# Starting the preparation of three attention units three steps later

## The chip, the cores and the metric

The kernel runs on one core of one Trainium2 chip. The time is the device time of that core in microseconds (us), the median of several executions. Five engines work beside each other, each through its own list of instructions in order: TensorE (PE in the profile), ScalarE (ACT), VectorE (DVE), GpSimd (POOL) and SyncE (SP), which here issues DMAs and DMA transposes. They wait for each other through semaphores.

## The reference

Normalised attention, then a feed-forward block with a residual, over 8 batches of 448 tokens, 12 heads of 64 and a model width of 768. Cut to what is computed:

```
q_n = q / sqrt(mean(q*q) + 1e-6) * g_q          (k_n likewise with g_k)
attn = softmax(q_n @ k_n.T / sqrt(64))
x = (attn @ v), heads side by side               (8, 448, 768), float32
xn = (x - mean(x)) / sqrt(var(x) + 1e-6) * g_ln
out = x + relu(xn @ w_ch1) @ w_ch2               w_ch1: 768 x 3072, w_ch2: 3072 x 768
```

## The kernel before, in words

**Pairs and units.** Attention works on pairs of heads: 48 pairs, six to a batch. The inputs of one or two pairs are loaded and prepared together as a unit. From unit 4 on a unit holds two pairs: unit 5 has pairs 8 and 9, unit 6 has 10 and 11, unit 7 has 12 and 13, unit 8 has 14 and 15, unit 9 has 16 and 17.

**Steps.** After a first stretch whose order is written out by hand, attention is a list of steps, numbered 7p + i for pair p and i = 0 to 6. Step 7p + i emits the scores of part i of pair p (S, lines 352 to 356, then the exponential on ScalarE at line 358) and the product with v of the pair before it (V, lines 381 and 383). The steps are dealt out among the chunks of the MLP of the batch before: an up chunk is six matmuls into psH (line 621) and a Relu on ScalarE (line 623); a down chunk is six matmuls into psC (line 637). While the MLP of batch 0 runs, it takes the steps up to 90 with it. The last 13 down chunks carry no steps; beside them the layer norm of the next batch is made on VectorE (lines 545, 560, 566) and transposed by DMA into xnT (line 593), which the up chunks of the next MLP read.

**Preparation of a unit.** It is cut into twelve pieces, which are put into the steps ahead of the scores of that step:

- `bai`: takes the buffers, squares k on ScalarE into the buffer khl (line 215), and multiplies k by the gains on GpSimd (line 229)
- `d`, `c`, `e`: sum of the squares of k on VectorE (line 218), squares of q on ScalarE into the buffer qn (line 215), their sum on VectorE
- `j`: the high half of k on ScalarE (line 237)
- `gv`: the roots on ScalarE (lines 221, 223), v on GpSimd
- `k`, `l`, `m`: the low half of k, the scaled q and its copy on VectorE (lines 240, 67, 279)
- `w`: the rest of v on GpSimd
- `x`, `y`, from unit 8 on: DMA transposes of khl and qn into kU and qU (lines 258, 261, 268, 271)

For units below 8, PE transposes khl and qn in place of `x` and `y`: K for pair p + 1 stands in step 7p + 2 (lines 313, 316) and Q for pair p + 1 in step 7p + 4 (lines 327, 330), both into one PSUM buffer tr, which VectorE copies out (lines 318, 335).

**Buffers.** khl and qn have two buffers each. A buffer that a unit takes is one that an earlier unit has been done with; its first writer is a square of ScalarE, which waits for the last reader of the earlier unit. The scores have two PSUM buffers psS: the scores of a step wait for the exponential of two steps before.

**Where the pieces stand.** A unit has a first step `st` and a last step `e`, and the ten pieces from `bai` to `w` are spread evenly between them; the rule and the table of exceptions:

```
st = max(7 * (p - 2 - m) + 2, last + 1, 7 * nb0)
e = max(7 * (p - 2) - 1, st + 5)
st, e = EARLY.get(u, (st, e))
...
at = st + (e - st) * x // (k - 1) if x < k else e + 1 + x - k
```

The order of PE, ScalarE, GpSimd and SyncE is that in which the steps emit; that of VectorE after the first stretch is chosen when the program is built. The load of the second half of `w_ch2` (`load_w2`, line 520, issued by GpSimd) is emitted in the step of unit 7's `bai`.

Of the kernel before, what the change touches and what calls it, by code (L numbers as in the profile page):

```python
# [45 lines left out]
""".split()  # L46
DMA_UNIT = 8
PE_SET = (DMA_UNIT + 1) % 2
EARLY = {5: (42, 49), 6: (47, 56)}
LN_EXP_SET = 6  # L50
UP_FIRST = 3
REC_LO, REC_HI = 1.0 / 3.0e7, 0.5
# [23 lines left out]
class _Fast:  # L76
# [381 lines left out]
    def attention(self):  # L458
# [3 lines left out]
        for u in range(4, nu):  # L462
            p, m = UNIT_PAIR[u], UNITS[u][2]
# [3 lines that stand above are left out]
            pieces = ["bai", "d", "c", "e", "j", "gv", "k", "l", "m", "w", "x", "y"]  # L467
# [469 lines left out]
```

## Time and profile before

| | |
|---|---|
| time, median of 3 | 615.18 us (614.29 to 615.19) |
| span of the profiled execution | 613.1 us |
| PE busy | 580.8 us (95%) |
| ScalarE, VectorE, GpSimd busy | 361.4, 286.8, 188.2 us |
| mean granted TensorE clock | 0.995 |

A line of a timeline has the start and the length in us, engine and source line, the operation, what it writes and reads, and in brackets the idle time of the engine ahead of it with what ended it. A line of the waits has who waited for whom: us in total, how often, the longest. A line of the windows has a stretch of time, and the busy time of each engine in it; PEclk is the share of full TensorE clock that was granted. PEld is the loading of weights, which overlaps PE.

### The profile page before, as it was taken

To read this page: it belongs to the slowest core of one execution; us is meant where nothing else is said; L and a number is where in the kernel's file an instruction comes from. 1 tells how busy PE (TensorE), PEld (TensorE's weight loads), DVE (VectorE), ACT (ScalarE), POOL (GpSimd) and SP (SyncE) were. 2 spreads that over 40 slices of the span, in tenths; PEclk is the share of its full clock that TensorE was granted. 3 is DMA by queue.
4 is the path that set the end of the run, shared out by engine and by line. 5 is a ranking of instruction groups with operands and counts; after the bars stand their busy time and mean duration, and the time that the engine had idled before them with its cause. 6 is when DMAs were issued, how large, how long until landed. Compare 5 with 4: busy or idle time off the path is not lost.

```text
span 613.1 us, 11532 instructions
## 1 busy us (share of the span) xinstructions
PE 580.8 (95%) x4500; PEld 346.3 (56%) x4500; DVE 286.8 (47%) x618; ACT 361.4 (59%) x697; POOL 188.2 (31%) x245
## 2 busy tenths in 40 slices
PE   2887999799999999999999999999999999999995
PEld 1555566455566666655566666655566666654564
DVE  5898566633356356643346355642355422440011
ACT  5996986338754498538755398537765377214200
POOL 2852621223452245514453145605322000000000
PEclk9999999899999999999999999999999999999999
DMA  9999999275766477847665496838523330030011
GB/s 193 272 212 207 213 221 189 31 222 134 122 109 128 117 123 150 180 106 144 105 108 141 107 136 151 176 104 151 119 59 87 91 61 2 27 104 0 1 52 56
DMA packets 130861, 75.29 MB, mean 123 GB/s; under 512 B 96656, under 2 KB 121040, under 8 KB 130800
## 3 DMA queue, kind: packets, MB, share of 16 engines
q1 hardware_dynamic: 114048, 45.12, 37.5%
q0 software_dynamic: 16080, 28.94, 21.1%
q8 instruction: 37, 0.61, 0.4%
q10 hardware_dynamic: 672, 0.43, 0.2%
q14 instruction: 24, 0.20, 0.1%
HBM read 52.36 MB, written 11.01 MB: 103 GB/s over the span
## 4 chain that ended last, share of the span: by engine, by line
PE 82%; DVE 2%; DMA 2%; ACT 2%; issue 1%; SPq 1%; DVEq 0%; ACTq 0%
PE psC L637 34%; PE psH L621 33%; PE psS L352 7%; PE oA L381 4%; PE oB L383 2%; PE psS L355 1%; PE psS L356 1%; DMA qkv<-in_k_dram 1%; DMA kU<-khl 1%; ACT E L358 1%; ACT qn L215 0%; DVE qn L67 0%; DVE stat L545 0%; DVE khl L240 0%; ACT khl L215 0%
## 5 line engine op out<-in xcount | busy, mean ns | idle before, releaser
L621 PE MATMUL psH<-xnT,w 128*128 128x512 f16 (+1 forms) x1134 | 241.9, 353 | 0.3 <-ACT hT L671 0.3
L637 PE MATMUL psC<-w,hT 128*128 128x384 f16 (+1 forms) x1368 | 235.6, 324 | 0.0
L358 ACT ACTIVATE E<-psS,rr_all 128x448 f16<-128x448 f32 x336 | 206.9, 635 | 47.8 <-PE psS L352 42.6
L623 ACT ACTIVATE hT<-psH 128x512 f16<-128x512 f32 (+1 forms) x189 | 104.1, 551 | 124.4 <-PE psH L621 121.6
L637 PEld LDWEIGHTS <-hT 128*128 128x128 f16 x1368 | 128.1, 98 | 74.8 <-issue 0.7
L621 PEld LDWEIGHTS <-w 128*128 128x128 f16 x1134 | 102.7, 98 | 81.2 <-issue 0.8
L352 PE MATMUL psS<-qU,kU 128*128 128x448 f16 x288 | 100.9, 358 | 10.9 <-ACT E L358 8.9
L381 PEld LDWEIGHTS <-E 128*128 128x128 f16 x1008 | 70.9, 98 | 51.0 <-issue 7.0
L229 POOL TENSOR_TENSOR qkv<-qkv,gprod 128x896 f32<-128x896 f32 x21 | 43.7, 2079 | 99.4 <-ACT khl L215 60.5
L381 PE MATMUL oA<-v,E 128*128 128x65 f16 x864 | 66.9, 194 | 0.1
L641 DVE SCALAR_TENSOR_TENSOR x<-psC,rs_all,x 128x384 f32<-128x384 f32 x48 | 28.9, 615 | 71.7 <-PE psC L637 71.2
L396 DVE RECIPROCAL rec_all<-oA 128x6 f32<-128x6 f32 x48 | 9.3, 194 | 96.6 <-PE oA L381 96.4
L383 PE MATMUL oB<-v,E 128*128 128x65 f16 x288 | 51.9, 194 | 0.1
L127 POOL DMA_DIRECT2D qkv<-in_k_dram x14 | 11.2, 797 | 129.7 <-ACT E L358 67.9
L218 DVE TENSOR_REDUCE ssq<-khl 128x14 f32<-128x896 f32 (+1 forms) x24 | 25.6, 1065 | 48.7 <-ACT khl L215 48.6
L352 PEld LDWEIGHTS <-kU 128*128 128x128 f16 x288 | 28.3, 99 | 24.6 <-issue 6.2
L218 DVE TENSOR_REDUCE ssq<-qn 128x14 f32<-128x896 f32 (+1 forms) x25 | 26.2, 1047 | 25.1 <-ACT qn L215 25.1
L67 DVE SCALAR_TENSOR_TENSOR qn<-qkv,rq 128x256 f16<-128x256 f32 (+1 forms) x72 | 26.5, 424 | 18.0 <-ACT rq L223 17.9
L383 PEld LDWEIGHTS <-E 128*128 128x128 f16 x336 | 32.5, 97 | 0.3 <-DVE xl L403 0.2
L398 DVE TENSOR_TENSOR x<-oA,rec_all 128x384 f32<-128x384 f32 x48 | 26.8, 558 | 1.5
L545 DVE BATCH_NORM_STATS2 stat<-x 128x6 f32<-128x256 f32 (+1 forms) x75 | 26.3, 405 | 0.7
L240 DVE TENSOR_TENSOR khl<-qkv,khl 128x896 f16<-128x896 f32 x21 | 22.8, 1087 | 7.1 <-ACT khl L237 6.3
(104 smaller groups left out, 446.7 us busy)
## 6 DMA issues: line engine op xcount, KB each, us to landing
out_dram<-x SPq DMA_DIRECT2D x20, 384.0 KB, 2.5
qkv<-in_k_dram POOLq DMA_DIRECT2D x14, 384.0 KB, 3.8
qkv<-in_q_dram POOLq DMA_DIRECT2D x14, 384.0 KB, 5.4
qkv<-in_v_dram POOLq DMA_DIRECT2D x14, 384.0 KB, 6.5
w<-in_moe_w_ch_dram POOLq DMA_DIRECT2D x3, 1536.0 KB, 14.5
w<-in_moe_w_ch_dram POOLq DMA_DIRECT2D x2, 2304.0 KB, 27.0
qkv<-in_k_dram SPq DMA_DIRECT2D x7, 384.0 KB, 5.7
qkv<-in_q_dram SPq DMA_DIRECT2D x7, 384.0 KB, 5.1
```

The costliest lines, as they stand in the source:

```text
L67: nc.vector.scalar_tensor_tensor(out=out, in0=x, scalar=8.0, in1=r.unsqueeze(2).broadcast_to([x.shape[0], g, D]), op0=ALU.mult, op1=ALU.mult)
L218: nc.vector.tensor_reduce(out=c["ssq"][:, n], in_=c["sq", n], axis=AX.X, op=ALU.add)
L229: (nc.vector if u in DVE_KG else nc.gpsimd).tensor_tensor(out=c["t"][1], in0=c["t"][1], in1=sh.gprod.unsqueeze(1).broadcast_to([128, g, D] ...
L352: nc.tensor.matmul(ps[:, 0:S], c["main"][:, ts(i, 128)], q[:, ts(h, S)], start=True, stop=True)
L358: nc.scalar.activation(out=c["E"][:, i], in_=ps[:, 0:S], func=AFT.Exp, scale=self.rr[:, g:g + 1], bias=EXP_BIAS)
L381: nc.tensor.matmul(oA[:, t, cs], E[:, i, ts(t, 128)], rhs, start=(i == 0 and t == 0), stop=(i == 6 and t == 2))
L383: nc.tensor.matmul(oB[:, cs], E[:, i, 320:448], rhs, start=(i == 0), stop=(i == 6))
L398: nc.vector.tensor_tensor(out=x[:, :, 128 * hp:128 * hp + 128].rearrange("p t (e d) -> p t e d", e=2), in0=oA[:, :, :, 0:D], in1=rec[:, 0: ...
L621: nc.tensor.matmul(ps[:, 0:N], sh.w1[:, dc, ts(f, 128)], xnT[:, dc, 0:N], start=(dc == 0), stop=(dc == NDC - 1))
L623: nc.scalar.activation(out=hT[:, f, 0:N], in_=ps[:, 0:N], func=AFT.Relu)
L637: nc.tensor.matmul(ps[:, 0:g[1]], hT[:, f, ts(t, 128)], sh.w2[:, f, cols], start=(f == 0), stop=(f == NFF - 1))
L641: nc.vector.scalar_tensor_tensor(out=x[:, cols], in0=ps[:, 0:g[1]], scalar=self.rs[:, b, t:t + 1], in1=x[:, cols], op0=ALU.mult, op1=ALU.add)
```

## The change

Units 7, 8 and 9 get an entry in the table of exceptions, each three steps after the rule's value, with the same last step. It is meant to put the first square behind the PE transposes that read the buffers which the unit takes, where before it stood ahead of them in the order of steps.

```diff
-EARLY = {5: (42, 49), 6: (47, 56)}
+EARLY = {5: (42, 49), 6: (47, 56), 7: (61, 69), 8: (75, 83), 9: (89, 97)}
```

The rule gave (58, 69), (72, 83) and (86, 97). So the pieces move as follows, and those of units 8 and 9 the same way 14 and 28 steps later:

| unit 7 | bai | d | c | e | j | gv | k | l | m | w |
|---|---|---|---|---|---|---|---|---|---|---|
| step before | 58 | 59 | 60 | 61 | 62 | 64 | 65 | 66 | 67 | 69 |
| step after | 61 | 61 | 62 | 63 | 64 | 65 | 66 | 67 | 68 | 69 |

The transposes K and Q of the pair 9 stand in steps 58 and 60, those of pair 11 in 72 and 74, those of pair 13 in 86 and 88. The pieces `x` and `y` of unit 8 stay in steps 84 and 85. No operation is added or taken away.

## The prediction

> **What bounds the kernel now.** I read the page first, then PE's waits in the stretch that holds steps 58 to 90 (about 71 to 116 us), then the timelines of ScalarE, PE and SyncE around the longest of them.
>
> ```profile
> PE 580.8 (95%) x4500; PEld 346.3 (56%) x4500; DVE 286.8 (47%) x618; ACT 361.4 (59%) x697; POOL 188.2 (31%) x245
> ...
> PE   2887999799999999999999999999999999999995
> ...
> PE psC L637 34%; PE psH L621 33%; PE psS L352 7%; PE oA L381 4%; PE oB L383 2%; PE psS L355 1%; PE psS L356 1%; DMA qkv<-in_k_dram 1%; DMA kU<-khl 1%; ACT E L358 1%; ACT qn L215 0%; DVE qn L67 0%; DVE stat L545 0%; DVE khl L240 0%; ACT khl L215 0%
> ```
>
> PE sets the end. It is full from the ninth slice to the end but the last, so a microsecond that PE loses before is a microsecond of the total. The seventh of the 40 slices above (92 to 107 us) is full, the eighth (107 to 123 us) is not: digit 7 stands there. PE's waits from 55 to 155 us:
>
> ```profile
> PE psS L352 <- ACT E L358: 3.5, 3, 2.7
> PE tr L327 <- DVE kU L318: 1.4, 2, 0.7
> PE psS L355 <- ACT E L358: 0.6, 2, 0.3
> ```
>
> One wait of 2.7 us carries most. Now the six squares of units 7, 8 and 9 in ScalarE's timeline:
>
> ```profile
> 72.41 0.95 ACT L215 ACTIVATE khl<-qkv 128x896 f32<-128x896 f32 x1 [0.21 <-PE tr L316]
> ...
> 75.37 0.95 ACT L215 ACTIVATE qn<-qkv 128x896 f32<-128x896 f32 x1 [0.20 <-PE tr L330]
> ...
> 89.10 0.95 ACT L215 ACTIVATE khl<-qkv 128x896 f32<-128x896 f32 x1
> ...
> 92.06 0.95 ACT L215 ACTIVATE qn<-qkv 128x896 f32<-128x896 f32 x1 [0.20 <-DMA qkv<-in_k_dram]
> ...
> 109.17 0.95 ACT L215 ACTIVATE khl<-qkv 128x896 f32<-128x896 f32 x1 [3.70 <-DMA kU<-khl]
> ...
> 112.86 0.95 ACT L215 ACTIVATE qn<-qkv 128x896 f32<-128x896 f32 x1 [1.69 <-DMA qU<-qn]
> ```
>
> Units 7 and 8 wait 0.2 us for PE's transposes; that is little. Unit 9 waits 3.7 us, and not for PE: K of pair 13 had ended at 106.7 us. It waits for the DMA transposes of unit 8, so unit 9 took the buffers of unit 8, which had been given back (steps 84, 85) ahead of those of unit 7 (K in step 86, Q in 88). SyncE's timeline shows these transposes[...]:
>
> ```profile
> 98.10 3.69 SPq L258 DMA_TRANSPOSE kU<-khl  x1
> 101.84 2.50 SPq L261 DMA_TRANSPOSE kU<-khl  x2
> 104.44 4.68 SPq L268 DMA_TRANSPOSE qU<-qn  x3
> 109.17 2.52 SPq L271 DMA_TRANSPOSE qU<-qn  x2
> ```
>
> The chain has the last landing of kU<-khl 5.96 us after 103.11, at 109.07, which is when the square begins. And PE:
>
> ```profile
> 106.88 1.14 PE L637 MATMUL psC<-w,hT 128*128 128x384 f16 x6
> 110.70 0.35 PE L352 MATMUL psS<-qU,kU 128*128 128x448 f16 x1 [2.68 <-ACT E L358]
> 110.89 0.25 PE L381 MATMUL oA<-v,E 128*128 128x65 f16 x3
> 110.97 0.19 PE L383 MATMUL oB<-v,E 128*128 128x65 f16 x1
> 111.86 0.27 PE L327 MATMUL tr<-id,qn 128*128 128x128 f16 x1 [0.69 <-DVE kU L318]
> 111.92 0.84 PE L330 MATMUL tr<-id,qn 128*128 128x128 f16 x6
> 112.56 2.12 PE L637 MATMUL psC<-w,hT 128*128 128x384 f16 x6
> ```
>
> The square stood in step 86 ahead of the exponential of S12.2. Blocked, it held up that exponential; the scores of step 88 wanted its psS buffer, and PE stood. The sum of the squares (VectorE, line 218) in turn stood ahead of the copy of tr, so Q of pair 13 came another 0.7 us late. And the six psC matmuls then took 1.92 us in the chain, not 0.97.
>
> **What the Trainium skill says.** "TensorE: Matmul & The Clock Gate", part 1, has the array at half clock after an idle window of about 3.4 us, and at full clock only after as long a busy one. The trace agrees: the windows give PEclk 0.50 from 112 to 115 us, after some 2.7 us of idleness and a broken microsecond. The same page, "Architectural detail", has ScalarE and VectorE as strict first-in first-out queues; here the blocked square held the exponential behind it. "ScalarE: Activation LUTs", "What ACT_TABLE_LOAD costs", prices an activation with immediate operands at 186 ns + 0.833 ns an element: 932 ns for 896, and the trace has 949.
>
> **The change part by part.**
>
> *Unit 9.* Its `bai` goes from step 86 to 89 and `c` from 88 to 90. The exponentials of S12.2, S12.3 and S12.4 then stand ahead of the square, so the scores of step 88 (buffer of S12.2), step 89 (S12.3) and step 90 (S12.4) find theirs free whatever the square waits for. The next scores, step 91, come after the 13 chunks without steps, 12.68 us later. So the wait is not taken away but has nobody behind it. What PE does between the end of psC at 107.85 us and the first of those chunks at 115.92 took 8.07 us. At full clock and without waits, from equal pieces in the chain: S 0.19, V 0.12, Q 0.41, psC 0.97, S and V 0.31, the split scores and V of step 90 0.61; 2.61 us in all. Gain 5.46 us: 2.85 of the first gap, 0.8 of the second, the rest slow clock and small gaps.
>
> *Units 7 and 8.* The squares leave the places before S8.2, S8.4, S10.2 and S10.4. Two short waits of PE follow on qn squares (0.28 at 76.89 us, 0.27 at 93.58 us). Gain 0.55 us.
>
> *What comes closer together.* Unit 7's two squares and the high half, each 0.84 us of ScalarE when queued closely, now stand in steps 61, 62 and 64 in place of 58, 60 and 62. ScalarE was busy 4.80 of 5 us from 75 to 80. Going through its queue from 72 us with an exponential at 0.52, a Relu at 0.37: it falls about 2 us behind at S9.1 and catches up by S9.4, with scores of steps 62 to 67 each finding their buffer free by 0.1 to 0.6 us. So 0 to 1 us of new stalls; I take 0.3. Unit 8's run stands where PE does down chunks, which need no Relu (ScalarE 3.28 of 5 us from 95 to 100), and costs nothing. The copy of tr for pair 12 may fall behind unit 8's low half on VectorE; 0 to 0.4 us, taken in the 0.3.
>
> *The rest of the preparation* ends in the same step or one later. Its readers are far: K of pair 12 in step 79, S14.0 in step 98. The `w_ch2` load is issued about 3 us later, from 75.5 to some 78.5, behind the first half that was still filling the queue (24 us to landing); its first user is the second column half of psC, at about 111 us, some 4 us after the landing at 106.8 (issue done at 77.0, 30 us to landing). Nothing.
>
> *The layer norm of batch 1.* It hangs on V of step 90, so it moves up with PE. Before, V ended at 115.9, the transposes into xnT were issued up to 125.2 and the last landed about 126.5; PE wanted it at 128.4. Slack 1.9 us. After: unit 8's transposes go one step (1.2 us) later, kU landing at about 110.3; square to 111.2, its sum on VectorE to 112.3; if that stands ahead of the copies out of step 90 (ready at 110.5), the chain starts 1.8 us late, inside the slack. 0 to 1.5 us; I take 0.2.
>
> Sum: 615.18 - 5.46 - 0.55 + 0.3 + 0.2 = 609.67 us. From 130 us on PE is full (69.87 of 70 us from 130 to 200), so nothing gives it back.
>
> **The rivals.**
>
> *The layer norm becomes the wait.* If VectorE also has unit 9's second sum ahead of the copies of step 90, the chain waits for the landing of qU<-qn, 112.8 + 1.2 = 114.0, plus square 0.95 and sum 1.1: copies at 116.0, as before. xnT lands at 126.6, PE stands from 123.0 to 126.6 and starts slow (about 1.6 us, as above). Gain 0.2 to 1.8: 613.8 us. For it: VectorE's order is chosen at build. Against: before, the low half of unit 9 was ready in time and still stood behind the whole layer norm.
>
> *The wait moves with the square.* PE stands in step 89 or 90 as it did in 88; only the 0.55 us remain: 614.6 us. For it: unit 9 would still take unit 8's buffers. Against: the count of psS buffers above.
>
> *Slower: the denser burst.* Unit 7 stalls PE for 1 us, the layer norm waits 3.6 us with 1.6 us of slow clock, and unit 8 adds 0.6 by the copy of tr: 5.46 + 0.55 - 6.8 = -0.8, and 616 us. For it: ScalarE's 96% from 75 to 80 us. Against: all three must come together.
>
> **How the numbers follow.** Forecast 0.75, layer norm 0.12, moved wait 0.07, slower 0.06. The forecast's own bounds are 609.2 (no new stall) to 611.7 (1 and 1.5 us of them); the median before moved by 0.9 us between executions, so the low end is 608.6. Above 613.4 lie the moved wait, the slower case and half the layer-norm case, 0.19. Faster by 0.2% means under 613.95: 0.75 and over half of 0.12, 0.82. Same 0.09, slower 0.09.
>
> **What would show it.** Right: no wait of PE for ScalarE over 0.5 us near 105 to 112 us; PEclk 1.00 there; unit 9's first square about 109 to 111 us, with a wait or none; first psH of 128x512 at about 122.6 to 123.2 us. ScalarE's squares of unit 7 at about 75.5 and 77.3 us. Wrong: PE waiting for xnT before that psH, a wait of psS for E in steps 61 to 67 over 0.5 us, or a new gap after 130 us.

## The result, and the profile after

| | before | after |
|---|---|---|
| time, median of 4 (us) | 615.18 (614.29 to 615.63) | 609.68 (608.87 to 610.34) |
| ratio, 95% interval | | 0.9912 [0.9893, 0.993] |
| span of the profiled execution (us) | 613.1 | 608.4 |
| part of the chain that PE carries | 82% | 88% |

The change takes 5.5 us off; the forecast was 609.7. First the page of after, with the lines that answer to those of before, and the clock:

```profile
PE 579.9 (95%) x4500; PEld 346.0 (57%) x4500; DVE 286.4 (47%) x618; ACT 360.5 (59%) x697; POOL 188.8 (31%) x245
...
PE   2886999999999999999999999999999999999995
...
PEclk9899999999999999999999999999999999999999
...
PE 88%; ACT 1%; DVE 0%; issue 0%; ACTq 0%
```

The eighth slice, which had a 7, is full. The clock of that slice was an 8 in the page of before and is a 9 here. The chain has lost its DMA share (2% before, none listed now). What is left of idle PE lies in the first four slices and the last; in the second this execution has a slow stretch of clock of its own, to which I come back.

PE's waits in the same stretch as before, 55 to 155 us, in the trace of after (total, times, longest):

```profile
PE psS L352 <- ACT E L358: 0.8, 2, 0.6
PE tr L327 <- DVE kU L318: 0.7, 1, 0.7
PE tr L313 <- DVE xnT L608: 0.7, 1, 0.7
PE psH L621 <- ACT hT L671: 0.3, 1, 0.3
```

All four lie before 70 us. From 70 to 155 us the list is empty, where before it held 2.7, 0.7 and 0.6 us, the stand in step 88 among them.

ScalarE's timeline of after: the squares of units 7, 8 and 9, and the exponentials around unit 9's:

```profile
76.52 0.95 ACT L215 ACTIVATE khl<-qkv 128x896 f32<-128x896 f32 x1
...
78.25 0.97 ACT L215 ACTIVATE qn<-qkv 128x896 f32<-128x896 f32 x1
...
92.95 0.95 ACT L215 ACTIVATE khl<-qkv 128x896 f32<-128x896 f32 x1
...
94.44 0.94 ACT L215 ACTIVATE qn<-qkv 128x896 f32<-128x896 f32 x1
...
109.14 0.94 ACT L215 ACTIVATE khl<-qkv 128x896 f32<-128x896 f32 x1
110.28 0.63 ACT L358 ACTIVATE E<-psS,rr_all 128x448 f16<-128x448 f32 x1 [0.20 <-PE psS L352]
114.32 0.95 ACT L215 ACTIVATE qn<-qkv 128x896 f32<-128x896 f32 x1 [3.40 <-DVE stat L560]
115.18 0.62 ACT L358 ACTIVATE E<-psS,rr_all 128x448 f16<-128x448 f32 x1
```

The square of k still starts at 109.1 us, as before (109.17), but the exponentials of the scores that PE needs are through. The square of q waits 3.40 us, longer than before (1.69). So the wait for the buffer of q has not gone. It costs nothing now, and PE's timeline of after shows why:

```profile
107.24 1.14 PE L637 MATMUL psC<-w,hT 128*128 128x384 f16 x6
108.22 0.35 PE L352 MATMUL psS<-qU,kU 128*128 128x448 f16 x1
...
108.92 1.14 PE L637 MATMUL psC<-w,hT 128*128 128x384 f16 x6
...
110.20 0.35 PE L355 MATMUL psS<-qU,kU 128*128 128x448 f16 x1
...
110.81 12.84 PE L637 MATMUL psC<-w,hT 128*128 128x384 f16 x78
123.48 1.46 PE L621 MATMUL psH<-xnT,w 128*128 128x512 f16 x6
```

At 110.81 PE begins the 78 matmuls of the 13 chunks without steps. It asks nothing of ScalarE for 12.67 us, and by then the square, at 114.32, is long done. The releaser named at that square, VectorE's `stat`, is the event that the profile saw last, and I take it for a bystander. SyncE's timeline has the transposes out of qn, which hold the buffer, issued up to about 113.1:

```profile
99.69 3.12 SPq L258 DMA_TRANSPOSE kU<-khl  x1
102.86 2.51 SPq L261 DMA_TRANSPOSE kU<-khl  x2
105.47 5.12 SPq L268 DMA_TRANSPOSE qU<-qn  x3
110.64 2.51 SPq L271 DMA_TRANSPOSE qU<-qn  x2
115.21 5.21 SPq L593 DMA_TRANSPOSE xnT<-xn  x4
```

The last two take some 1.25 us each to issue, so the last began at about 111.9; with the median of 2.5 us from issue to landing (96 to 126 us) my estimate of its landing is 114.4, when the square begins. The trace of e8 below, whose square stands in the same place, names the wait as `DMA qU<-qn` (3.04 us), and so do those of e2, e4, e5 and e7; e1 has a `stat`, as here.

**Where the time came from.** PE executes the same 4500 matmuls in the same order in before, after and every experiment. So the start of one and the same matmul can be compared between two traces. The shift is its start minus that in before, in us; the three right-hand columns are differences of shifts, that is, what a stage gained (negative) or lost.

| kernel | at 58.0 | K of pair 9 (71.8) | K of pair 13 (106.1) | chunks without steps (115.7) | first psH of batch 1 (128.4) | pair 9 to 13 | pair 13 to chunks | chunks to psH |
|---|---|---|---|---|---|---|---|---|
| after | 0.96 | 0.95 | 0.37 | -4.95 | -4.95 | -0.58 | -5.32 | 0.00 |
| e1_only9 | -0.12 | -0.13 | -0.13 | -5.45 | -5.45 | 0.00 | -5.32 | 0.00 |
| e2_only78 | 1.28 | 1.28 | 0.71 | 0.13 | 0.13 | -0.57 | -0.58 | 0.00 |
| e3_other_place | 1.52 | 1.53 | 1.53 | -2.82 | -2.82 | 0.00 | -4.35 | 0.00 |
| e4_nine87 | 1.83 | 1.34 | 1.34 | -2.92 | -1.57 | 0.00 | -4.26 | 1.35 |
| e5_nine88 | 1.73 | 1.23 | 1.23 | -4.09 | -4.08 | 0.00 | -5.32 | 0.01 |
| e6_q_later | 1.79 | 1.28 | 1.28 | -0.70 | -0.70 | 0.00 | -1.98 | 0.00 |
| e7_k_later | 1.87 | 1.87 | 1.86 | 0.77 | 1.65 | -0.01 | -1.09 | 0.88 |
| e8_load_58 | 0.15 | 0.15 | -0.44 | -5.76 | -5.75 | -0.59 | -5.32 | 0.00 |

From the first psH to the end no shift moves by more than 0.03 us. The first column concerns the stretch ahead of all edits; it is taken up at the end.

### The profile page after: what moved, and what is told of

It is laid out like the page before. It is cut to its first block, busy times and chain, and to the rows that moved or that the text cites. A ratio compares the mean times of both kernels' runs of the same rounds, so it can differ in the third digit from the quotient of the medians.

```text
span 608.4 us, 11527 instructions
## 1 busy us (share of the span) xinstructions
PE 579.9 (95%) x4500; PEld 346.0 (57%) x4500; DVE 286.4 (47%) x618; ACT 360.5 (59%) x697; POOL 188.8 (31%) x245
## 4 chain that ended last, share of the span: by engine, by line
PE 88%; ACT 1%; DVE 0%; issue 0%; ACTq 0%
PE psC L637 36%; PE psH L621 35%; PE psS L352 8%; PE oA L381 5%; PE oB L383 2%; PE psS L356 1%; PE psS L355 1%; ACT E L358 0%; PE tr L330 0%; PE tr L316 0%; ACT khl L215 0%; ACT qn L215 0%; ACT khl L237 0%; ACT hT L623 0%; DVE x L398 0%
```

## The experiments

Theory A is that of the prediction: nearly all of the gain is unit 9's. Its blocked squares no longer stand ahead of an exponential that PE waits for, though the wait itself, for unit 8's DMA transposes, stays. The rivals are named in each expectation. The first four kernels were timed beside the kernel before on one chip, where it took 615.54 us, the other four on a second chip, where it took 615.53.

**e1_only9: unit 9 alone.**

```diff
-EARLY = {5: (42, 49), 6: (47, 56)}
+EARLY = {5: (42, 49), 6: (47, 56), 9: (89, 97)}
```

> Unit 9 alone is moved, to (89, 97); units 7 and 8 stand as before. Theory A (one stand: unit 9's square of k waited for the DMA transposes of unit 8, whose buffer it takes, and held up an exponential that PE wanted): nearly the whole gain, 609.7 to 610.5 us, no wait of PE for ScalarE over 0.5 us from 104 to 112 us. Theory B (each unit's squares were held by the PE transposes of the buffers, so each unit brings a third): about 613.3 us. Theory C (the load of the second half of w_ch2, which moves with unit 7, makes the DMA transposes land earlier): about 615 us.

Measured: 610.06 us (609.72 to 611.45), ratio 0.9912 [0.9888, 0.9935]. From 70 to 155 us PE has these waits left, the two short ones behind the squares of q of units 7 and 8, which have not moved:

```profile
PE psS L355 <- ACT E L358: 0.6, 2, 0.3
```

The stage of unit 9 gains 5.32 us, exactly as in after. One entry of three is the whole of the change, as far as timing can tell.

**e2_only78: units 7 and 8 alone.**

```diff
+EARLY = {5: (42, 49), 6: (47, 56), 7: (61, 69), 8: (75, 83)}
```

> Units 7 and 8 alone are moved; unit 9 stands at (86, 97) as before. Theory A: the stand of PE in step 88 is still there, 2 to 4 us long, followed by slow clock; two waits of 0.3 us are gone; 614.5 to 616 us. Theory B: two thirds of the gain, about 611.5 us. Theory C: the whole gain, about 610 us.

Measured: 615.56 us (614.79 to 617.46), ratio 1.0003 [0.999, 1.0016]. The two units gain 0.57 us, as in after. Then the stands come. PE's timeline of e2:

```profile
110.41 0.35 PE L352 MATMUL psS<-qU,kU 128*128 128x448 f16 x1 [1.69 <-ACT E L358]
...
111.57 0.22 PE L327 MATMUL tr<-id,qn 128*128 128x128 f16 x1 [0.69 <-DVE kU L318]
...
115.29 0.35 PE L355 MATMUL psS<-qU,kU 128*128 128x448 f16 x1 [1.88 <-ACT E L358]
```

The first is 1.69 us in place of 2.68, less than the 2 to 4 expected, and no slow clock follows: PEclk is 1.00 in every microsecond from 104 to 116. In their place there is another stand, of 1.88 us in step 90, behind the square of q, which waits 2.88 us for `qU<-qn`. From 58 us to the chunks the profiled execution gains 1.15 us (its shift goes from 1.28 to 0.13), while the medians are equal; in this execution the late start takes the gain back. What takes it back in the others, no trace shows.

**e3_other_place: unit 9's squares written to a place that nobody else holds.** All pieces stay in the steps of before.

```diff
             c["sq", n] = o.rearrange("p (g d) -> p g d", d=D)
+            if u == 9:
+                c["sq", n] = self.hT[:, 0:14, 384:512].bitcast(FP32)
```

> All pieces stand as before, but unit 9's squares are written to columns of hT that batch 0 leaves unused, so they wait for no DMA transpose. The tracking of hT by ranges ties the square to the psC chunk before it and the next chunk to the square, which may cost PE up to 0.5 us. Theory A: the stand is gone without any piece moved, 609.9 to 611 us, the square of k at about 106 us. Theory B: the place in the steps is what counts, about 615 us. Theory C: about 615 us as well.

Measured: 611.46 us (610.89 to 612.3), ratio 0.9926 [0.9904, 0.9949]. The square of k, the scores of step 88 and the psC chunk after them in the trace of e3 (its lines stand two further down in the file):

```profile
107.59 0.95 ACT L217 ACTIVATE hT<-qkv 128x896 f32<-128x896 f32 x1 [0.58 <-DMA kU<-khl]
...
109.58 0.35 PE L354 MATMUL psS<-qU,kU 128*128 128x448 f16 x1
...
111.03 1.15 PE L639 MATMUL psC<-w,hT 128*128 128x384 f16 x6 [0.58 <-ACT hT L217]
```

The square starts at 107.59; without the 1.53 us by which this execution is late, that is the 106 us expected. It no longer needs the landing that is named beside it, since it writes to hT; the psC chunk ahead of it, which reads hT, ends at about the same time. PE no longer stands in step 88, though no piece has moved. So it was the buffer that made the square wait, and not its step. The stage gains 4.35 us and not 5.32: the borrowed place lies in hT, and two psC chunks start late behind the squares written into it, by 0.2 and 0.7 us.

**e4_nine87: unit 9 one step later, not three.**

```diff
+EARLY = {5: (42, 49), 6: (47, 56), 9: (87, 97)}
```

> Unit 9 alone is moved, by one step, to (87, 97): the square of k then stands ahead of the exponential of S12.3 and behind that of S12.2. Theory A with the count of psS buffers: the square still waits until about 109 us, but PE wants that exponential's buffer only in step 89, about 109.9 us; a stand of 0.4 to 1 us, no slow clock, 610.1 to 611.2 us. If the gain went with the number of steps moved, a third of it: about 613.4 us. Theory B: about 615 us, since K of pair 13 is passed but Q is not.

Measured: 613.17 us (612.25 to 616.04), ratio 0.9967 [0.9953, 0.9981]. That is 2 to 3 us slower than theory A expected: a miss. The square of k now stands behind K of pair 13, the last reader of unit 7's buffer, which ended at 108.07 us. It waits all the same, and for the transposes of unit 8:

```profile
110.19 0.95 ACT L215 ACTIVATE khl<-qkv 128x896 f32<-128x896 f32 x1 [1.95 <-DMA kU<-khl]
```

The wait of PE in step 89 is a small one, as it should be; with the short gaps behind it, it costs 1.06 of the 5.32 us. But PE's timeline of e4 has a new wait, far from any score:

```profile
111.71 0.35 PE L352 MATMUL psS<-qU,kU 128*128 128x448 f16 x1 [0.68 <-ACT E L358]
...
112.84 8.94 PE L637 MATMUL psC<-w,hT 128*128 128x384 f16 x54
122.97 2.27 PE L637 MATMUL psC<-w,hT 128*128 128x384 f16 x13 [1.19 <-DVE x L641]
```

PE waits for VectorE to add a finished psC to x. VectorE's timeline of e4 shows why VectorE is late:

```profile
114.44 1.09 DVE L218 TENSOR_REDUCE ssq<-qn 128x14 f32<-128x896 f32 x1 [1.66 <-ACT qn L215]
115.45 0.19 DVE L396 RECIPROCAL rec_all<-oA 128x6 f32<-128x6 f32 x1
...
118.53 2.81 DVE L566 SCALAR_TENSOR_TENSOR xn<-x,stat,gln 128x768 f16<-128x768 f32 x3
121.25 1.02 DVE L566 SCALAR_TENSOR_TENSOR xn<-xl,stat,gln 128x768 f16<-128x768 f32 x1
122.30 1.67 DVE L641 SCALAR_TENSOR_TENSOR x<-psC,rs_all,x 128x384 f32<-128x384 f32 x3
```

In this build the sum of q's squares stands ahead of the layer norm. Its square waited for `qU<-qn`, so the layer norm starts at 115.45 although PE had given V at about 113.0 (112.78 + 0.22), and the additions from psC come after it all. That is the prediction's layer-norm rival, real and in another form: PE runs short of psC buffers, and not of xnT. The loss is 1.35 us, from the chunks to psH. In this execution another 1.1 us come from a stretch of slow clock from 56 to 60 us, ahead of the edit (see the end).

**e5_nine88: unit 9 two steps later.**

```diff
+EARLY = {5: (42, 49), 6: (47, 56), 9: (88, 97)}
```

> Unit 9 alone at (88, 97): squares of k in step 88 and of q in step 90, the sum of the squares of q in step 91. Theory A: the square of k stands behind the exponential of S12.3, and PE wants that of S12.4 only in step 90, about 110.2 us; a stand of at most 0.6 us, and VectorE's sum of q is out of the way of the layer norm: 609.9 to 611.2 us. If it is VectorE's sum of k ahead of the layer norm that cost the kernel with unit 9 at (87, 97) its 2 us, this one loses them too: 612 to 613.5 us.

Measured: 611.21 us (610.63 to 611.84), ratio 0.9935 [0.9915, 0.9954]. Nothing is lost behind the chunks, and the stage gains 5.32 us, as in after. As the sum of k still stands ahead of the layer norm here, and that of q behind it, the loss in e4 hangs on the sum of q. The median lies 1.1 us above e1's; this execution was 1.36 us later than e1's at pair 9, before unit 9 begins, 1.1 of it by the same stretch of slow clock as in e4.

**e6_q_later: unit 9 as before, but the square of q in step 90 and its sum in step 91.**

```diff
+                at = {"c": 90, "e": 91}.get(names, at) if u == 9 else at
```

> Unit 9's k pieces stand as before (square in step 86); only the square of q and its sum go to steps 90 and 91. Theory A: PE's stand in step 88 is untouched, 2 to 3 us and 0.7 behind it, with or without slow clock after; 612.5 to 615 us. If the square of q alone were what counts: about 610 us.

Measured: 614.59 us (611.42 to 617.03), ratio 0.998 [0.9966, 0.9994]. PE's waits of e6 from 70 to 155 us:

```profile
PE psS L352 <- ACT E L358: 2.3, 1, 2.3
PE tr L327 <- DVE kU L318: 0.7, 1, 0.7
PE psS L355 <- ACT E L358: 0.5, 2, 0.3
```

Both stands of before are still there, so it is the square of k in step 86 that makes them. The stage gains 1.98 us nevertheless: the first stand is 0.35 us shorter, and the clock stays full behind the two, in the windows of e6 (PEclk is the third figure from the right):

```profile
112.00:114.00 2.00, 1.31 (x17) 0.89 (x13) 1.36 (x3) 0.64 (x2) 1.25 (x1) 1.00 0.09 17
114.00:116.00 2.00, 2.00 (x19) 1.31 (x18) 0.73 (x3) 1.46 (x3) 1.25 (x3) 1.00 0.00 0
```

**e7_k_later: the square of q in step 88, that of k in step 89.** It turns the two round, to set the waits of q and k against each other.

```diff
+            if u == 9:
+                pieces = ["b", "c", "e", "ai", "d", "j", "gv", "k", "l", "m", "w", "x", "y"]
...
+                if u == 9 and x < k:
+                    at = (88, 88, 89, 89, 89, 92, 93, 94, 95, 96, 97)[x]
```

> The reverse: unit 9's square of k and its sum go to step 89, the square of q and its sum stay in 88 and 89. Theory A read from the times of the landings: with the first stand gone ScalarE comes to the square of q at about 108 us and waits for qU<-qn until 112.8 to 114; the exponential of S12.4 stands behind it and PE wants it in step 90, a stand of 3 to 4 us, 613 to 615.5 us. Theory A read from the idle times before (3.70 us for k, 1.69 for q): most of the gain is k's, 610 to 611.5 us.

Measured: 617.49 us (613.93 to 619.08), ratio 1.0031 [1.0019, 1.0044]: slower than the kernel before. The direction is that of the reading by landing times, whose range it leaves by 2 us. ScalarE's timeline of e7 has the square:

```profile
113.92 0.95 ACT L215 ACTIVATE qn<-qkv 128x896 f32<-128x896 f32 x1 [4.46 <-DMA qU<-qn]
```

The exponential of step 88's scores is behind it, PE stands 3.58 us in step 90, and the clock follows, in the windows of e7:

```profile
112.00:114.00 2.00, 0.00 (x0) 0.00 (x0) 0.00 (x0) 0.08 (x1) 0.00 (x0) 1.00 0.09 17
114.00:116.00 2.00, 0.56 (x2) 0.26 (x2) 1.10 (x2) 2.00 (x3) 0.00 (x0) 0.71 0.00 0
116.00:118.00 2.00, 2.00 (x10) 1.19 (x9) 1.94 (x5) 1.28 (x3) 1.64 (x1) 0.50 0.00 0
```

The gain is gone. That e7 is slower than before is another matter: by the table its stages come to 0.2 us less than before (-1.09 and 0.88), and the profiled execution was 1.87 us late at 58 us, ahead of the edit. The clock has a part in it: the two executions of e7 with a mean clock of 0.999 took 613.93 and 614.89 us, the two such of before on the same chip 613.86 and 614.43, and most of e7's others ran at 0.988 to 0.994, most of before's at 0.995.

In before, the wait of q's square (1.69 us) looked the lesser of the two. It was short only because the wait for k in front of it, 3.70 us, had used up the time. The landing decides, at about 113 to 114 us in these traces: a square that stands in a step before it waits until then, whatever the trace of another order shows as its idle time.

**e8_load_58: the change, with the load of `w_ch2` left in step 58.**

```diff
-                    todo[at].append(lambda u=u: self.load_w2(u - 6))
+                    todo.setdefault(58 if u == 7 else at, []).append(
+                        lambda u=u: self.load_w2(u - 6))
```

> The whole change, but the load of the second half of w_ch2 stays in step 58. Theory A: as the change, 609.2 to 610.5 us. Theory C (the later load helps or harms): away from it by over 1 us, seen in the landing of kU<-khl.

Measured: 609.83 us (609.1 to 610.61), ratio 0.9913 [0.9894, 0.9933]. The stages are those of after to 0.01 us. The later load is worth nothing, neither a loss nor a gain. The times of after, e1 and e8 can't be told apart, and none of the experiments beat them.

## Why the prediction was right

**Unit 9.** Forecast 5.46 us, measured 5.32. The first gap gave the 2.85 us forecast (shift 0.37 at K of pair 13, -2.48 at the scores of step 88), the second 0.85 for 0.8 (shift -3.33 at Q of pair 13), and the rest 1.62 for 1.81. The 0.14 us that are missing are a slip in the forecast's 8.07 us. It runs from 107.85, when the next matmul could have started, to 115.92, when the matmul ahead of the chunks had ended; the chunks themselves start at 115.76, so the stretch was 7.91 us. The work in it took 2.60 us in after, for 2.61. That the buffers were what the squares waited for is shown by e3: with another place for the squares the stand is gone. That they are unit 8's, and not unit 7's, is shown by e4, whose square stands behind K of pair 13 and still waits for the landing of `kU<-khl`. So for unit 9 the aim of the change, to get behind the PE transposes, is not what brings the gain. That the wait itself is not removed is shown by the 3.40 us at q's square in after. The landing of kU was forecast 1.2 us later than before, at 110.3. It came earlier: the transposes were issued 1.6 us later, yet k's square starts at 109.14 with no idle time ahead of it. The median from issue to landing was 4.5 us in place of 6.0, from 96 to 126 us.

**The slow clock.** The forecast counted part of the 5.46 us as slow clock, and rested on the half clock after an idle window that the Trainium skill gives ("TensorE: Matmul & The Clock Gate", part 1). A window of before and two of after agree, with 0.50 in the first and full clock in the others:

```profile
112.00:114.00 2.00, 2.00 (x12) 1.30 (x11) 0.16 (x1) 1.14 (x2) 0.33 (x1) 0.50 0.01 0
...
112.00:114.00 2.00, 2.00 (x14) 1.22 (x13) 1.94 (x8) 0.00 (x0) 1.59 (x4) 1.00 0.13 26
114.00:116.00 2.00, 2.00 (x14) 1.17 (x12) 2.00 (x6) 1.65 (x4) 0.00 (x0) 1.00 0.00 0
```

What the slow clock cost can be read from the starts: from Q of pair 13 to the first of the chunks the same matmuls took 3.90 us in before (111.86 to 115.76) and 2.28 in after (108.53 to 110.81), as in e6. So 1.62 of the 5.32 us are clock. The prediction's "the trace agrees" holds for the half clock and not for the length: the page's window is about 3.4 us, the longest stand there was 2.68, and e6 after 2.33 us kept full clock.

**Units 7 and 8.** Forecast 0.55 us of gain, measured 0.58 in after, 0.57 and 0.59 in e2 and e8. In the total of the timed runs it can't be seen: e1 without it is as fast.

**The denser burst.** Forecast a loss of 0.3 us, measured none: from 70 to 120 us of after PE is busy 5.00 of 5 us in each of ten windows, though ScalarE fills 4.97 of 5 from 80 to 85. The squares of unit 7 come at 76.52 and 78.25; without the late start of 0.96 us that is 75.6 and 77.3, as forecast. So the term was too dear by 0.3 us, within the bounds of 0 to 1 that it was given.

**The layer norm.** The forecast allowed for the sum of k ahead of the copies of step 90, and left the sum of q behind them. VectorE's timeline of after has just that:

```profile
110.11 1.08 DVE L218 TENSOR_REDUCE ssq<-khl 128x14 f32<-128x896 f32 x1 [0.37 <-ACT khl L215]
111.12 0.19 DVE L396 RECIPROCAL rec_all<-oA 128x6 f32<-128x6 f32 x1
...
119.02 1.08 DVE L218 TENSOR_REDUCE ssq<-qn 128x14 f32<-128x896 f32 x1
```

PE's V had ended at 110.97, so nearly nothing is lost. The last transpose into xnT is issued from 119.2 us on; with the median of 2.5 us my estimate of its landing is 121.7. PE wants it at 123.48. That leaves 1.8 us of slack, against 1.9 before. The 0.2 us put down for it were not needed.

**The load.** Forecast nothing, and e8 shows nothing.

**The rivals.** The wait did move with the square of q, but after has nobody behind it; e4 and e7 show what a wait costs where somebody is, stands of 0.68 us in step 89 and of 3.58 in step 90. The layer norm as the wait was put at 0.12; it is what e4 runs into, one step earlier than the change, while the change itself escapes it because its sum of q stands behind the layer norm. The slower case did not come about. The order that is slower than before, e7, loses its gain in another way, by a square of q ahead of an exponential.

**What is partly luck.** The stages of after sum to 5.32 + 0.58 = 5.90 us, for 6.01 forecast before losses; the medians differ by 5.50, for 5.5 forecast. In the profiled pair 4.95 us of the 5.90 are left, since at 58 us, ahead of all that the change moves, the execution of after is 0.96 us later than that of before, with a slow stretch of clock from 22 to 26 us. That the forecast's two small losses, 0.5 us that did not come, make up for what the start takes is chance. Two more things were left to chance: the build put the sum of q behind the layer norm, where in e4 it put it ahead; and the 1.62 us of clock can be gained only where stands bring the slow clock, which those of e2 and e6 did not.

## What to carry to other kernels

When a pool has two buffers, find out which earlier user gives its buffer back first, by the trace and not by the numbering: it is that user's last reader that the new one waits for, as unit 9 waited for unit 8's transposes and not for unit 7's. A wait that can't be taken away is free where nobody stands behind it in its engine's queue, so count the buffers between the engine that waits and the one that sets the end, and put the waiting instruction just before the stretch in which they don't meet. The idle time ahead of a waiting instruction does not tell what it will wait in another order; the time of the landing does.

## What the runs showed of the hardware that was not expected

- **The length of a stand does not tell whether the slow clock follows.** In before, PE stood 2.68 and 0.69 us with short work between, and the clock was at 0.50 from 112 to 114 us. In e6, 2.33 and 0.69 us left it at 1.00, and so did e2's 1.69, 0.69 and 1.88. In e7, 3.58 us brought 0.71, 0.50 and 0.94 in the three windows of 2 us from 114 us on. Nor is a long stand needed: from 46 to 56 us PE has the same gaps in before, e4, e5 and e6, each to 0.01 us and none over 0.75. In e4, e5 and e6 the clock is at 0.50 from 56 to 58 us and at 0.66 to 0.69 from 58 to 60, which costs 1.1 us; in before it is at 1.00 throughout. What decides between the two, these traces do not show.
- **The start differs from trace to trace without cause in the code.** The first 58 us run the same instructions in the same order on each engine, yet the shift there goes from -0.12 to 1.87 us. In five traces most of it is clock: in after and e7 there is a stretch of slow clock from 22 to 26 us (0.50 and 0.71, 0.67 and 0.50), in e4, e5 and e6 the one from 56 to 60 us. But e2 and e3 come 1.28 and 1.52 us late with 1.00 in every window up to 60 us. The timed medians follow the start in part: the stages of e5 sum to -5.3 us, its median is 4.3 us below before. Whether it belongs to the kernel as built or to the execution is open, since each kernel has one trace, and with it the order of after, e5 and e1 among themselves.
- **The time to landing of a transpose differs from trace to trace.** The transposes out of khl land 6.0 us after their issue in before, 4.5 us in after, 5.6 in e8 and 6.7 in e1 (medians of three, 96 to 126 us), those into xnT 2.5 us in all four. What it depends on, no run sets apart. SyncE takes about 1.25 us to issue one of the small ones (lines 261 and 271), and 3.1 to 3.7 us for that of line 258.
